# First MLP layer of a fused attention and MLP kernel: blocks of 512 tokens against whole batches

## The chip, the cores and the metric

One core of one Trainium2 chip. The metric is device time of one execution in microseconds; three runs of the kernel before took 1290.98, 1290.95 and 1288.83 us (median 1290.95).

## The reference, cut to what matters

Eight batches of 576 tokens, 512 channels, all float32. Three stages follow each other.

```
a   = softmax(phi, axis=seq)                       # 32 memories a head, 8 heads
k_m, v_m = a^T k, a^T v                            # per head 32 x 64
x   = softmax(q k_m^T / 8) v_m                     # attention output, 576 x 512 a batch
y   = x + relu(LN(x) @ w_ch1) @ w_ch2              # 512 -> 2048 -> 512: the MLP of this change
h   = gelu(y @ w_in); u, v = halves of h           # the second MLP ("phase two")
out = y + (u * (w_sg @ LN(v) + b_sg)) @ w_out
```

The weights w_ch1 and w_ch2 come as float64 and are converted on the chip.

## The kernel before, in words

Float32 products are made of three fp32r matmuls (high by high, high by low, low by high), so each operand exists as a pair of tiles, h and l. Because x is attention weights times v_m, the first layer is not computed from x: `make_vw` multiplies v_m of a batch with the centred, scaled w_ch1 (tiles VW, per batch b and block fb of 512 hidden units), and layer one multiplies VW with the attention weights aT directly. So layer one's stationary operand depends on the batch. The division by the standard deviation of x comes at the end, as a factor of the row.

**Tokens and tiles.** Two batches (a pair) make nine tiles of 128 tokens: four of the even batch, one that joins the last 64 tokens of both, four of the odd batch (`tile_rows`, L125). `phase1` runs the 36 tiles in nine blocks of four, 512 tokens. A block's aT has two tiles of 512 columns.

**Steps.** A block has 16 steps, one for each chunk c of 128 hidden units. In a step `m1` (L549) does layer one for 512 tokens into one PSUM bank ph (two such banks, L137), in pieces where the batch changes within the block (`pieces`, L537): every piece has six matmuls. Relu goes to ScalarE (hh, L563), its low part to VectorE (hl, L564). Two steps later `m2` (L567) does layer two: four tiles of 128 tokens, each three matmuls of 512 columns into a PSUM bank y0 to y3 that collects over the 16 steps (L574 to L576). After the last step VectorE scales a bank, adds x (L579) and the tile goes to y_d in DRAM.

**What sets the order.** All other work of phase one is a list of calls with due times in steps (`at_time`, L587); `run_until` issues what is due between m1 and m2 of a step. `tile_base` (L591) gives the times of the attention units: a unit (batch b, 128 tokens i, the last one 64) lays q out in DRAM (`lay_q`), loads it, transposes it on VectorE (`t_q`, L328), makes scores on TensorE (`t_scores`, L337), softmax (`t_norm`) and aT (`t_attn`). `t_x` (L442) multiplies aT with v_m for the residual x, `t_ln` takes its statistics. Batch 0's first four units run ahead of step 0 in a form of their own (`t_q0`, `t_scores0`, `t_attn0`, two units at a time). A planner under the kernel orders the instructions of each engine by its own estimate of times; all DMAs are issued on SP's queue, in order.

**Weights and room.** Raw W1 and W2 chunks and the converted W2 (16 tiles) share `wpool`, 22 tiles of 4 KB a partition; VW and the centred W1 share `wpool2`, 13 tiles, with part of VW in wpool for odd batches.

**The end of phase one.** From the last block on, `begin_phase2(n)` (L823) prepares phase two, n steps into that block: w_sg is transposed from n = 0, w_in is loaded from n = 3, w_out from n = 11, y of pair 0 comes back from DRAM from n = 9 (`y_in`), and `s2` (L786), the first product of phase two, runs for its first five tiles from n = 12. In the last block the chunks are taken in the order 12 to 15, 0 to 11, so that wpool2 comes free early. `s2` and the w_sg transposes take turns in two PSUM banks (tag v).

Of the kernel before, what the change touches and what calls it, by code (L numbers as in the profile page):

```python
# [28 lines left out]
def fused_kernel(ctx: ExitStack, tc: tile.TileContext, q, k, v, phi, g1, w1, w2, w_in, g2, w_sg, b_sg, w_out, out):  # L29
# [7 lines left out]
    P = 128  # L37
# [30 lines left out]
    es_mlp, es_w2, es_attn, es_right, es_left = ExitStack(), ExitStack(), ExitStack(), ExitStack(), ExitStack()  # L68
# [66 lines left out]
    def phase1():  # L135
# [6 lines left out]
        wpool2 = pool(es_w2, "wpool2", 13)  # L142
# [55 lines left out]
        def lay_q(u, b, i):  # L198
# [4 lines left out]
            for a in range(4):  # L203
                src = q[b].rearrange("(c o) s (e f) -> o e s c f", o=2, e=2)
                with behind_w2(TB <= u["T"]["t"] < 2 * TB, 6 + u["T"]["t"] - TB):
                    load(t[a, 0:u["n"]], src[a // 2, a % 2, i * P:min((i + 1) * P, S)])

        def load_q(u, b, i):
            n = u["n"]
            if u["T"]["t"] < TB:  # L210
# [3 lines left out]
                load(t, q[b, :, i * P:(i + 1) * P, :].rearrange("h p d -> p h d"))  # L214
# [146 lines left out]
        def t_q0(us):  # L361
            qTs = two(wpool, F32, "qT0")
            for u, qT in zip(us, qTs):
                t = u.pop("q")
                u["qT"] = qT = qT.rearrange("p (c n) -> p c n", c=4)
                pt = ps_0([P, 4, P], "ptq")
                for pr in range(4):
                    PE.transpose(pt[:, pr, :], t[:, 2 * pr:2 * pr + 2, :].rearrange("p h d -> p (h d)"), ident)
                A.copy(qT, pt)

        def t_scores0(us):
            kT = st["kT"]
            sc = ps_0([P, 2, 2, P], "sc")
# [11 lines left out]
            z, a = two(wpool, F32, "z0")  # L385
            V.transpose(out=z, in_=sc.rearrange("p t g n -> p (t g n)"))
            z3 = z.rearrange("p (b m) -> p b m", m=NM)
            m = at.tile([P, 16], F32, tag="m0", name="m0")
            V.tensor_reduce(out=m, in_=z3, axis=AX.X, op=ALU.max)
            V.tensor_tensor(out=z3, in0=z3, in1=m.unsqueeze(2).to_broadcast([P, 16, NM]), op=ALU.subtract)  # L390
            A.activation(z, z, AF.Exp, scale=SCALE)
            us[0]["z"] = (z, z3, a)

        def t_attn0(us):
            z, z3, a = us[0]["z"]
            r = at.tile([P, 16], F32, tag="r0", name="r0")
# [3 lines left out]
            V.tensor_tensor(out=z3, in0=z3, in1=r.unsqueeze(2).to_broadcast([P, 16, NM]), op=ALU.mult)  # L400
            tr = V.transpose(out=a, in_=z)
            if 0 not in aT:
                aT[0] = (
                    mo.tile([P, HK, BLK], F32R, tag="aTh", name="aTh"),
                    mo.tile([P, HK, BLK], F32R, tag="aTl", name="aTl"),
                )
            a3 = a.rearrange("p (t g n) -> p g t n", t=2, g=2)
            t0 = us[0]["T"]["t"]
            ah, al = (x[:, :, t0 * P:(t0 + 2) * P].rearrange("p g (t n) -> p g t n", t=2) for x in aT[0])
            A.copy(ah, a3)  # L410
            lo = (G if t0 == 0 else V).tensor_tensor(out=al, in0=a3, in1=ah.bitcast(F32), op=ALU.subtract)
            for u in us:
                u["T"]["tr"] = tr if t0 == 0 else lo
# [11 lines left out]
        def t_attn(u):  # L425
# [5 lines left out]
            j, tt = divmod(u["T"]["t"], TB)  # L431
            if j not in aT:
                aT[j] = (
                    mo.tile([P, HK, BLK], F32R, tag="aTh", name="aTh"),
                    mo.tile([P, HK, BLK], F32R, tag="aTl", name="aTl"),
                )
            ah, al = aT[j]
            cs = slice(tt * P + u["o"], tt * P + u["o"] + n)
# [3 lines left out]
        def t_x(T):  # L442
            j, tt = divmod(T["t"], TB)
            ah, al = aT[j]
            ts_ = slice(tt * P, (tt + 1) * P)
            T["x"] = mo.tile([P, DM], F32, tag="x", name="x", bufs=8)
            for o, m, b, _ in tile_rows(*divmod(T["t"], TPP)):
                VBh, VBl = VBs[b % 2]
                px = ps_a.tile([P, DM], F32, tag="a", name="px")
                for g in range(HK):  # L450
                    cs = slice(g * 4 * D, (g + 1) * 4 * D)
# [530 lines left out]
```

## Time and profile before

| | |
|---|---|
| three runs | 1288.83, 1290.95, 1290.98 us; median 1290.95 |
| profiled execution | span 1287.4 us from its first to its last instruction |
| TensorE busy | 1230.4 us, 96% of the span |
| VectorE, ScalarE, GpSimd busy | 679.6, 440.6, 408.6 us |
| mean granted clock of TensorE | 0.981 |
| layer one (L559) | 1536 matmuls |
| layer two (L574 to L576) | 1728 matmuls |

The profile is of one execution, taken by the hardware. Busy time is the union of an engine's instructions; matmuls overlap, so the time one of them costs is the distance from its start to the next start. The granted clock is a share of full speed: TensorE runs at 2.4 GHz (1.00) or 1.2 GHz. The time of the profiled execution itself is its span; the runs' times include what lies around the span.

### The profile page before, as it was taken

The numbers are of one execution on the slowest core, as the hardware profiler recorded it, in microseconds if no ns is written. First come the engines' busy times: TensorE is split into PE (matmuls) and PEld (weight loads), VectorE is DVE, ScalarE is ACT, GpSimd is POOL, SyncE is SP. The second block draws the span as 40 slices with busy tenths as digits, with TensorE's granted clock in tenths as the row PEclk, the third lists the DMA queues.
The fourth block names the chain that finished last, engine by engine and source line by source line (L and its number), as shares of the span: only waits on it lengthen the run. The fifth ranks groups of instructions, "written<-read, shape, count | busy, mean of one in ns | idle before, by whom it ended". The sixth has DMA issues, their size and how long they took to land.

```text
span 1287.4 us, 20559 instructions
## 1 busy us (share of the span) xinstructions
PE 1230.4 (96%) x7723; PEld 1024.8 (80%) x7723; DVE 679.6 (53%) x1472; ACT 440.6 (34%) x870; POOL 408.6 (32%) x659
## 2 busy tenths in 40 slices
PE   4589989999999999999999999999999999999998
PEld 2367667888878888788787888778998998998997
DVE  3677564445355355345354434765567547547632
ACT  2653332222223232132132123543353444434430
POOL 1144222111102111111021112514575666647641
PEclk8689989999999999999999999999999999999999
DMA  9996673164353453532431104322033024013301
GB/s 213 305 259 162 188 189 91 52 182 123 100 146 99 117 142 89 146 106 79 136 83 58 51 25 136 123 84 75 25 91 106 1 80 134 9 34 115 91 9 66
DMA packets 205076, 138.96 MB, mean 108 GB/s; under 512 B 95536, under 2 KB 176688, under 8 KB 204976
## 3 DMA queue, kind: packets, MB, share of 16 engines
q1 hardware_dynamic: 204976, 137.64, 38.4%
q8 instruction: 61, 1.00, 0.3%
q14 instruction: 39, 0.32, 0.1%
HBM read 114.53 MB, written 31.46 MB: 113 GB/s over the span
## 4 chain that ended last, share of the span: by engine, by line
PE 84%; DMA 7%; DVE 4%; SPq 2%; issue 1%; ACT 1%; POOL 1%; POOLq 0%; DVEq 0%; ACTq 0%
PE ph L559 17%; PE py L574 9%; PE py L576 9%; PE pvs L891 9%; PE py L575 9%; PE po L914 8%; PE pu L866 7%; PE pv L794 6%; DMA raw<-in_moe_w_ch_dram 4%; PE pvw L515 2%; PE sc L342 2%; SPq L80 2%; PE kvp L276 1%; DMA kv<-in_v_dram 1%; PE px L452 1%
## 5 line engine op out<-in xcount | busy, mean ns | idle before, releaser
L559 PE MATMUL ph<-aTh,vw 128*128 128x64 f32 (+7 forms) x1024 | 254.1, 318 | 10.2 <-ACT aTh L410 4.6
L574 PE MATMUL py<-whl,hh 128*128 128x512 f32 x576 | 230.3, 403 | 0.0
L575 PE MATMUL py<-whl,hh 128*128 128x512 f32 x576 | 227.5, 395 | 0.0
L576 PE MATMUL py<-whl,hl 128*128 128x512 f32 x576 | 225.6, 395 | 0.0
L559 PEld LDWEIGHTS ph<-aTh,vw 128*128 128x128 f32 x1024 | 178.2, 191 | 33.3 <-issue 7.5
L564 DVE SCALAR_TENSOR_TENSOR hl<-ph,hh 128x512 fp32r<-128x512 f32 x144 | 99.0, 687 | 169.8 <-ACT hh L563 169.5
L563 ACT ACTIVATE hh<-ph 128x512 fp32r<-128x512 f32 x144 | 86.0, 599 | 266.2 <-PE ph L559 264.9
L559 PE MATMUL ph<-aTl,vw 128*128 128x448 f32 (+7 forms) x512 | 163.7, 320 | 0.0
L574 PEld LDWEIGHTS py<-whl,hh 128*128 128x128 f32 x576 | 108.6, 188 | 30.0 <-issue 6.3
L576 PEld LDWEIGHTS py<-whl,hl 128*128 128x128 f32 x576 | 108.3, 188 | 27.9 <-issue 5.1
L421 POOL TENSOR_TENSOR z<-z,r 128x256 f32<-128x256 f32 (+1 forms) x36 | 20.5, 570 | 342.7 <-DVE r L420 278.7
L575 PEld LDWEIGHTS py<-whl,hh 128*128 128x128 f32 x576 | 108.6, 189 | 20.9 <-issue 2.1
L891 PE MATMUL pvs<-wsh,vhl 128*128 128x288 f32 x576 | 121.2, 294 | 0.0
L559 PEld LDWEIGHTS ph<-aTl,vw 128*128 128x128 f32 x512 | 97.7, 191 | 16.0 <-issue 8.6
L866 PE MATMUL pu<-yTh,whl 128*128 128x288 f32 x512 | 110.4, 295 | 0.0
L794 PE MATMUL pv<-whl,yTh 128*128 128x512 f32 x288 | 91.9, 400 | 3.8 <-DVE vg L784 3.8
L891 PEld LDWEIGHTS pvs<-wsh,vhl 128*128 128x128 f32 x576 | 94.3, 188 | 0.6
L914 PE MATMUL po<-whl,gh 128*128 128x512 f32 x288 | 90.8, 391 | 0.0
L866 PEld LDWEIGHTS pu<-yTh,whl 128*128 128x128 f32 x512 | 85.0, 188 | 1.0
L866 PE MATMUL pu<-yTl,whl 128*128 128x288 f32 x256 | 75.4, 295 | 0.0
L891 PE MATMUL pvs<-wsl,vhl 128*128 128x288 f32 x256 | 75.4, 295 | 0.0
L894 POOL TENSOR_TENSOR gt<-gt,ug 128x288 f32<-128x288 f32 x64 | 51.6, 808 | 63.7 <-DVE gt L893 62.8
(161 smaller groups left out, 2079.0 us busy)
## 6 DMA issues: line engine op xcount, KB each, us to landing
wc<-w_d SPq DMA_DIRECT2D x56, 512.0 KB, 4.9
y_d<-x SPq DMA_DIRECT2D x36, 256.0 KB, 3.9
yr<-y_d SPq DMA_DIRECT2D x36, 256.0 KB, 3.0
kv<-in_k_dram SPq DMA_DIRECT2D x32, 256.0 KB, 4.3
kv<-in_v_dram SPq DMA_DIRECT2D x32, 256.0 KB, 4.4
raw<-in_moe_w_ch_dram SPq DMA_DIRECT2D x32, 256.0 KB, 9.6
raw<-in_moe_w_ch_dram SPq DMA_DIRECT2D x16, 512.0 KB, 8.2
out_dram<-yr SPq DMA_DIRECT2D x32, 256.0 KB, 2.0
```

The costliest lines, as they stand in the source:

```text
L80: return nc.sync.dma_start(out=out_ap, in_=in_ap)
L559: PE.matmul(ph[:, c0:c1], w[:, ks], x[:, g, c0:c1], start=(n == 0), stop=(n == 3 * HK - 1))
L563: A.activation(hh, ph, AF.Relu)
L564: st["hl"] = V.scalar_tensor_tensor(out=hl, in0=ph, scalar=0.0, in1=hh.bitcast(F32), op0=ALU.max, op1=ALU.subtract)
L574: PE.matmul(py, hh[:, ts_], wh, start=start, stop=False)
L575: PE.matmul(py, hh[:, ts_], wl, start=False, stop=False)
L576: PE.matmul(py, hl[:, ts_], wh, start=False, stop=stop)
L794: PE.matmul(pv, y[:, kc, cs], w, start=(n == 0), stop=(n == 3 * KC - 1))
L866: PE.matmul(pu, w[:, ds_], y[:, kc, cs], start=(n == 0), stop=(n == 3 * KC - 1))
L891: PE.matmul(pvs, v_, w_, start=(n == 0), stop=(n == len(ops) - 1))
L894: G.tensor_tensor(out=gt, in0=gt, in1=ug, op=ALU.mult)
L914: PE.matmul(po, gg[:, dc, cs], w, start=(n == 0), stop=(n == 3 * KC - 1))
```

## The change

Layer one and two go by batches: eight blocks of 576 tokens instead of nine of 512. A step's layer one has two pieces, of 256 and 320 tokens, each in a PSUM bank of its own (the same two banks). The first 512 tokens of a batch go on to layer two as before, as four tiles. The outputs of the last 64 tokens are kept (`rems`, four tiles of wpool a pair, for 16 chunks), the even batch's in columns 0 to 63, the odd batch's in 64 to 127; when the odd batch is done, `m2_rem` does layer two for the joined tile, 48 matmuls into one bank. In the last pair these matmuls are spread over the last block's steps, in a bank of tag v.

With it: batch 0's last 64 tokens are attended ahead of step 0, as a third group; t_x stands within the batch's own block (x has seven buffers, was eight); the due times of units, W1 and W2 change; VW lies in `wearly` (6 tiles) and `wlate` (2), the centred W1 in `wcen` (5); the last block takes its chunks in plain order, and phase two's preparation begins at n = 3 instead of 0, y_in at 12 instead of 9, s2 at 13 instead of 12.

```diff
-        wpool2 = pool(es_w2, "wpool2", 13)
+        wlate = pool(es_w2, "wlate", 2)
+        wearly = pool(es_wc, "wearly", 6)
+        wcen = pool(es_wc, "wcen", 5)
...
-                h, l = two(wpool if b % 2 and fb < NFB - 1 else wpool2, F32R, "vw")
+                h, l = two(wearly if fb < NFB - 1 else wlate, F32R, "vw")
...
-        def t_x(T):
...
-            T["x"] = mo.tile([P, DM], F32, tag="x", name="x", bufs=8)
-            for o, m, b, _ in tile_rows(*divmod(T["t"], TPP)):
...
+        def t_x(T, b, i):
+            ah, al = aT[b]
+            VBh, VBl = VBs[b % 2]
+            o, n = (0, P) if i < 4 else (REM * (b % 2), REM)
+            ts_ = slice(i * P - o, i * P + n)
+            if "x" not in T:
+                T["x"] = mo.tile([P, DM], F32, tag="x", name="x", bufs=7)
...
+        hid, ybank, rems = {}, {}, {}
+        PIECES = ((0, 2 * P), (2 * P, S))
+
+        def m1(b, c):
+            ah, al = aT[b]
             fb, n = divmod(c, DM // P)
             ks = slice(n * P, (n + 1) * P)
-            ph = ps_h.tile([P, BLK], F32, tag="h", name="ph")
-            for c0, c1, b in pieces(j):
+            pair, odd = divmod(b, 2)
+            if not odd and c % 4 == 0 and (pair, c // 4) not in rems:
+                rems[pair, c // 4] = wpool.tile([P, 4, 2, P], F32R, tag="w", name="rem")
+            rem = rems[pair, c // 4][:, c % 4, :, REM * odd:REM * odd + REM]
+            hh = mo.tile([P, BLK], F32R, tag="hh", name="hh", bufs=3)
+            hl = mo.tile([P, BLK], F32R, tag="hl", name="hl", bufs=3)
+            for c0, c1 in PIECES:
+                ph = ps_h.tile([P, S - 2 * P], F32, tag="h", name="ph")[:, 0:c1 - c0]
                 n = 0
                 for g in range(HK):
                     wh, wl = VW[b, fb][g]
                     for w, x in ((wh, ah), (wh, al), (wl, ah)):
-                        PE.matmul(ph[:, c0:c1], w[:, ks], x[:, g, c0:c1], start=(n == 0), stop=(n == 3 * HK - 1))
+                        PE.matmul(ph, w[:, ks], x[:, g, c0:c1], start=(n == 0), stop=(n == 3 * HK - 1))
                         n += 1
-            A.activation(hh, ph, AF.Relu)
-            st["hl"] = V.scalar_tensor_tensor(out=hl, in0=ph, scalar=0.0, in1=hh.bitcast(F32), op0=ALU.max, op1=ALU.subtract)
-            hid[j, c] = (hh, hl)
+                outs = [(ph[:, 0:2 * P], hh[:, c0:c0 + 2 * P], hl[:, c0:c0 + 2 * P])]
+                if c1 == S:
+                    outs.append((ph[:, 2 * P:], rem[:, 0, :], rem[:, 1, :]))
+                for src, h, l in outs:
+                    A.activation(h, src, AF.Relu)
+                    st["hl"] = V.scalar_tensor_tensor(out=l, in0=src, scalar=0.0, in1=h.bitcast(F32), op0=ALU.max, op1=ALU.subtract)
+            hid[b, c] = (hh, hl)
...
+        def m2_rem(pair, c, bank):
+            if c == 0:
+                ybank["rem", pair] = bank()
+            py = ybank["rem", pair]
+            rem = rems[pair, c // 4]
+            wh, wl = W2[c]
+            PE.matmul(py, rem[:, c % 4, 0, :], wh, start=(c == 0), stop=False)
+            PE.matmul(py, rem[:, c % 4, 0, :], wl, start=False, stop=False)
+            PE.matmul(py, rem[:, c % 4, 1, :], wh, start=False, stop=(c == NF - 1))
+            if c == NF - 1:
+                t = TPP * pair + 4
+                y_of(py, tiles[t], t)
+
+        rems[0, 0] = wpool.tile([P, 4, 2, P], F32R, tag="w", name="rem")
...
+        def unit_base(b, i):
+            if b == 1:
+                return B1 + (0, 1.6, 2.6, 3.6, 4.4)[i]
+            if b == 2:
+                return 16.2 + 2.6 * i
+            return 16 * b - 18.1 + 3 * i - 0.5 * (i == 4)
...
+                x0, dx = (16 * b + 2.3, 0.25) if b == B - 1 else (16 * b + 2.4, 2)
+                at_time(x0 + dx * i, t_x, u["T"], b, i)
...
-            at_time(4 * fb - 18.5 if fb > 1 else 0.3 * fb - 26.5, load_w1, fb)
-            at_time((-16.5, -5.5, 2.6, 6.6)[fb], scale_w1, fb)
-            at_time((-16.4, -0.6, 4.0, 8.0)[fb], center_w1, fb)
-            at_time((-15, 0.8, 5.1, 9.1)[fb], make_vw, 0, fb)
+            at_time((-26.5, -26.2, -10.5, -4.5)[fb], load_w1, fb)
+            at_time((-16.5, -5.5, 1.6, 4.6)[fb], scale_w1, fb)
+            at_time((-16.4, -0.6, 2.6, 6.0)[fb], center_w1, fb)
+            at_time((-15, 0.8, 4.1, 7.6)[fb], make_vw, 0, fb)
         for c in range(NF):
-            at_time(1.1 * c - 16 if c > 2 else 0.2 * c - 26.4, load_w2, c)
+            at_time(c - 8.6 if c > 8 else 1.1 * c - 16 if c > 2 else 0.2 * c - 26.4, load_w2, c)
...
-        LAST = [*range(12, NF), *range(12)]
-        steps = [(j, c if j < NB - 1 else LAST[c]) for j in range(NB) for c in range(NF)]
+        LAST = NF * (B - 1)
+        steps = [(b, c) for b in range(B) for c in range(NF)]
+        rem_steps = list(range(NF))
...
-                m2(*steps[n - LAG], (n - LAG) % NF == 0, (n - LAG) % NF == NF - 1)
+                b, c = steps[n - LAG]
+                m2(b, c)
+                if b % 2 and b < B - 1 and c == NF - 1:
+                    for c in range(NF):
+                        m2_rem(b // 2, c, lambda: ps_y.tile([P, DM], F32, tag="y0", name="pyr"))
             run_until(n + 0.99)
-            begin_phase2(n - NF * (NB - 1))
+            begin_phase2(n - LAST)
+            for _ in range(2):
+                if n - LAST >= 4 and rem_steps and rem_steps[0] <= n - LAST - LAG:
+                    m2_rem(NPAIR - 1, rem_steps.pop(0), lambda: R["ps"].tile([P, DM], F32, tag="v", name="pyr", bufs=2))
...
-        if n == 0:
+        if n == 3:
             es_attn.close()
...
-        if n == 5:
-            es_w2.close()
+        if n == 12:
+            es_wc.close()
             R["py"] = pool(es_right, "p1y", 1, side="right")
...
-            if n == 9 + (2 * t) // 3:
+            if n == 12 + t // 2:
                 y_in(pairs[0], t)
-            if t < 5 and n == 12 + t:
+            if t < 5 and n == 13 + t:
                 s2(pairs[0], t)
```

## Rows read from the trace of the kernel before

**Rows 1.** Table of stretches: us, busy (x instructions) per engine, granted clock, DMA share, GB/s.
```profile
0.00:82.00 82.00, 44.44 (x255) 27.70 (x256) 47.95 (x87) 40.78 (x72) 13.13 (x27) 0.82 0.98 260
82.00:150.00 68.00, 67.27 (x403) 48.79 (x402) 43.66 (x87) 27.83 (x53) 27.83 (x33) 0.97 0.72 206
150.00:180.00 30.00, 22.69 (x194) 14.52 (x194) 19.36 (x53) 7.17 (x16) 9.26 (x13) 0.83 0.60 141
180.00:778.00 598.00, 596.67 (x4010) 488.79 (x4009) 274.44 (x642) 155.13 (x315) 89.32 (x187) 1.00 0.38 103
778.00:868.00 90.00, 86.58 (x382) 69.02 (x380) 59.33 (x112) 42.46 (x92) 31.57 (x37) 1.00 0.39 118
...
sum 1287.40, PE 1230.41 PEld 1024.81 DVE 679.58 ACT 440.57 POOL 408.59; mean PE 205.07 PEld 170.80 DVE 113.26 ACT 73.43 POOL 68.10
```

**Rows 2.** The chain of waits by engine, shares of the span.
```profile
PE 84%; DMA 7%; DVE 4%; SPq 2%; issue 1%; ACT 1%; POOL 1%; POOLq 0%; DVEq 0%; ACTq 0%
```

**Rows 3.** Timeline of TensorE, one step in five blocks: start us, duration us, instruction.
```profile
313.92 0.22 PE L559 MATMUL ph<-aTh,vw 128*128 128x128 f32 x1
...
315.65 0.40 PE L574 MATMUL py<-whl,hh 128*128 128x512 f32 x1
...
367.57 0.25 PE L559 MATMUL ph<-aTh,vw 128*128 128x192 f32 x1
...
369.13 0.40 PE L574 MATMUL py<-whl,hh 128*128 128x512 f32 x1
...
452.77 0.28 PE L559 MATMUL ph<-aTh,vw 128*128 128x256 f32 x1
...
454.20 0.39 PE L574 MATMUL py<-whl,hh 128*128 128x512 f32 x1
...
729.77 0.36 PE L559 MATMUL ph<-aTh,vw 128*128 128x448 f32 x1
...
731.46 0.28 PE L559 MATMUL ph<-aTh,vw 128*128 128x64 f32 x1
731.57 0.47 PE L574 MATMUL py<-whl,hh 128*128 128x512 f32 x1
...
778.44 0.39 PE L559 MATMUL ph<-aTh,vw 128*128 128x512 f32 x1
...
779.80 0.39 PE L574 MATMUL py<-whl,hh 128*128 128x512 f32 x1
```

**Rows 4.** Costliest groups, layer one's matmuls: x count, busy us, mean ns, idle before.
```profile
L559 PE MATMUL ph<-aTh,vw 128*128 128x64 f32 (+7 forms) x1024 | 254.1, 318 | 10.2 <-ACT aTh L410 4.6
...
L559 PE MATMUL ph<-aTl,vw 128*128 128x448 f32 (+7 forms) x512 | 163.7, 320 | 0.0
```

**Rows 5.** Chain of waits in phase two, one s2: start us, us, what.
```profile
1057.06 2.80 PE pv L794 x12
```

**Rows 6.** Groups by line and shape, VectorE and ScalarE passes over PSUM.
```profile
L564 DVE SCALAR_TENSOR_TENSOR hl<-ph,hh 128x512 fp32r<-128x512 f32 x144 | 99.0, 687 | 169.8 <-ACT hh L563 169.5
...
L782 DVE SCALAR_TENSOR_TENSOR z<-z,pu 128x288 f32<-128x288 f32 x64 | 28.9, 452 | 58.4 <-ACT z L781 58.0
...
L563 ACT ACTIVATE hh<-ph 128x512 fp32r<-128x512 f32 x144 | 86.0, 599 | 266.2 <-PE ph L559 264.9 <-PE py L575 0.6
```

**Rows 7.** Layer one's line: what TensorE sat idle for ahead of it (us, times).
```profile
  DVE hl L564: 6.3, 6
```

**Rows 8.** Chain of waits between the first two blocks: start us, us, what.
```profile
154.90 1.05 DVE qT L332
...
163.39 1.07 DVE qT L332
...
169.34 5.04 DMA kv<-in_v_dram
```

**Rows 9.** Waits in the last block of phase one: us in total, times, longest.
```profile
PE pv L794 <- DVE vg L784: 3.6, 2, 2.8
```

**Rows 10.** DMA issues: x count, KB each, median us from issue to landing.
```profile
raw<-in_moe_w_ch_dram SPq DMA_DIRECT2D x16, 512.0 KB, 8.2
```

More of the change, by code (lines that the diff above doesn't have):

```diff
@@ L66, in fused_kernel @@
     g2c = const.tile([P, KC], F32, name="g2c")
-    es_mlp, es_w2, es_attn, es_right, es_left = ExitStack(), ExitStack(), ExitStack(), ExitStack(), ExitStack()
+    es_mlp, es_w2, es_wc, es_attn, es_right, es_left = (ExitStack() for _ in range(6))
     def pool(es, name, bufs, **kw):
@@ L484, in scale_w1 @@
         def scale_w1(fb):
-            WC[fb] = ws = [wpool2.tile([P, 2, DM], F32, tag="w", name="wc") for _ in range(2)]
+            WC[fb] = ws = [wcen.tile([P, 2, DM], F32, tag="w", name="wc") for _ in range(2)]
             for j, raw in enumerate(raws.pop(fb)):
@@ L501, in load_wc @@
         def load_wc(fb):
-            WC[fb] = [wpool2.tile([P, 2, DM], F32, tag="w", name="wc") for _ in range(2)]
+            WC[fb] = [wcen.tile([P, 2, DM], F32, tag="w", name="wc") for _ in range(2)]
             for n in range(2):
@@ L577, in m2 @@
                 if stop:
[L578 to L580 removed]
+                    y_of(py, tiles[full(b, t)], full(b, t))
+        def m2_rem(pair, c, bank):
[11 more added lines that the diff above has]
+        rems[0, 0] = wpool.tile([P, 4, 2, P], F32R, tag="w", name="rem")
         tiles = [{"t": t} for t in range(NPAIR * TPP)]
@@ L589, in at_time, with full @@
             seq[0] += 1
-        def tile_base(t):
-            j, r = divmod(t, TB)
-            if j == 0:
-                return -17.5 + 6 * (r // 2) + 0.1 * (r % 2)
-            if j == 1:
-                return B1 + r + 0.6 * (r > 0)
-            return 16 * j - 18.1 + 3 * r
-        first_us = []
-        for b in range(B):
-            pair, odd = divmod(b, 2)
-            t0 = pair * TPP
-            items = []
-            if odd:
-                items.append((t0 + 4, 4, REM, REM))
-                items += [(t0 + 5 + i, i, 0, P) for i in range(4)]
-            else:
-                items += [(t0 + i, i, 0, P) for i in range(4)]
-                items.append((t0 + 4, 4, 0, REM))
-            first = tile_base(items[0][0])
+        def full(b, i):
+            return TPP * (b // 2) + (5 * (b % 2) + i if i < 4 else 4)
+        def unit_base(b, i):
[4 more added lines that the diff above has]
+            return 16 * b - 18.1 + 3 * i - 0.5 * (i == 4)
+        for b in range(B):
+            odd = b % 2
+            first = -17.5 if b == 0 else unit_base(b, 0)
             f = {1: F1, 2: F1}.get(b, 1.0)
@@ new lines, in phase1 @@
+            us = [
+                {"seen": set(), "E": V if i == 0 and b == 1 else G, "n": P if i < 4 else REM, "b": b, "i": i, "T": tiles[full(b, i)]}
+                for i in range(5)
+            ]
+            for i, u in enumerate(us):
+                if b == 0:
+                    at_time(-27, load_q, u, b, i)
+                    if i % 2 == 1 or i == 4:
+                        group = us[i - i % 2:i + 1]
+                        at_time(-21 + 0.1 * i, t_q0, group)
+                        at_time(-17 + 0.1 * i, t_scores0, group)
+                        at_time(-16 + 0.1 * i, t_attn0, group)
+                else:
+                    base = unit_base(b, i)
+                    at_time(base - (5.5 if i < 4 else 4), lay_q, u, b, i)
+                    at_time(base - (3.5 if i < 4 else 2), load_q, u, b, i)
+                    at_time(base, t_q, u)
+                    f = 0.7 if b == 1 else 1.0
+                    at_time(base + f, t_scores, u)
+                    at_time(base + 2 * f, t_norm, u)
+                    at_time(base + 3 * f, t_attn, u)
+                x0, dx = (16 * b + 2.3, 0.25) if b == B - 1 else (16 * b + 2.4, 2)
+                at_time(x0 + dx * i, t_x, u["T"], b, i)
+                if i in (1, 3):
+                    at_time(x0 + dx * i + 0.2, t_ln, [us[i - 1]["T"], us[i]["T"]])
+                if i == 4 and odd:
+                    at_time(x0 + dx * i + 0.2, t_ln, [u["T"]])
```

166 lines of the change are left out of this document (60 added, 106 removed).

## The prediction

> **What bounds the kernel now.** I read the table of stretches first. Between 180 and 778 us TensorE is busy 596.7 of 598 us at full granted clock, VectorE 274.4, ScalarE 155.1 and the DMA engines 0.38; from 82 to 150 us it is 67.3 of 68, in the last block of layer one (778 to 868) 86.6 of 90 [rows 1]. Only the start up to 82 us and the stretch from 150 to 180 us (22.7 of 30 us busy, clock 0.83) are bound by something else. The chain of waits says the same: 84% of the span is TensorE, 7% DMA, 4% VectorE [rows 2]. So what counts is how long TensorE needs for the instructions that change, and whether it now waits at the seams.
>
> Busy time of a matmul is no price here, since matmuls overlap: a step of 12 matmuls with 256 columns takes 1.43 us from its first start to the start of the next line, though one lasts 0.28 us. I take starts from the timeline [rows 3]. One step of layer one (six matmuls, or six and six) costs 1.36 us with 512 columns (778.44 to 779.80), 1.43 with 256+256 (452.77 to 454.20), 1.56 with 192+320 (367.57 to 369.13), 1.73 with 128+384 (313.92 to 315.65) and 1.80 with 448+64 (729.77 to 731.57). The last 64-column matmul and the next instruction are 0.11 us apart (731.46 to 731.57). 512 columns take 1.36/6 = 0.227, so 64 columns cost half of that, not an eighth: narrow pieces pay a floor.
>
> **The change part by part.** *Layer one.* Before, nine blocks of 512 tokens run 16 steps each: two blocks in one piece of 512, two each of 448+64, 384+128, 320+192, one of 256+256. That is 16 x (2 x (1.36 + 1.80 + 1.73 + 1.56) + 1.43) = 16 x 14.33 = 229.3 us, in 1024 + 512 = 1536 matmuls [rows 4]. After, 8 batches x 16 steps x 12 are again 1536 matmuls, over the same columns, but all 256 or 320 wide. Six of 256 cost half of 1.43, 0.715. Six of 320 are 1.56 less six of 192; with 192 held at the floor of 0.11 that is 0.89; by proportion between 256 and 512 columns it is 0.715 + 0.645 x 64/256 = 0.876. I take 0.89: 128 x 1.605 = 205.4 us, so **-23.9 us** (ends: -25.7 with 0.876, and -22, since one step a block is read and 0.015 us a step is 2 us in all). It lies on TensorE's dense stretches, so it is on the path; against 512 or 256+256 a step grows by 0.25 or 0.17 us, against the rest it shrinks.
>
> *Layer two.* 36 tiles x 48 matmuls of 512 columns stand before and after (8 batches x 4 tiles, and 4 joined tiles). A joined tile puts 48 into one PSUM bank in a row. Twelve into one bank take 2.80 us in phase two [rows 5], 0.233 each against 0.227: 192 x 0.006 = **+1.2 us**.
>
> *Evictions.* One pair (Relu on ScalarE, subtraction on VectorE) a step becomes three: 256, 256 and 64 columns. VectorE takes 0.687 us for 512 and 0.452 for 288 columns [rows 6], so about 0.15 + 0.00105 a column: 0.42 + 0.42 + 0.22 = 1.06 us. In all 128 x 1.06 = 135 against 99.0 us, +36 us; ScalarE (0.599 for 512) grows likewise. With VectorE 46% busy in the main stretch this is hidden, at nothing; if the cover went, 0.37 us a step would show. The new wait is on the two PSUM banks of layer one: a bank was used every second step, now every step, so a piece must be evicted within the other piece (0.9 us) and layer two (12 x 0.227 = 2.7 us), 3.6 us. The bare eviction is 0.6 + 0.7 us. TensorE waited for this subtraction 6.3 us in six places in the whole run [rows 7]. Behind a waiting matmul all of TensorE stands, layer two included. 0 to +6, I take **+1**.
>
> *Batch 0's last 64 tokens* move ahead of the first step: one q load of 128 KB (0.5 us at the 260 GB/s of the first 82 us [rows 1]), four transposes, four score matmuls, some nine small VectorE passes. The load stands on SP's queue ahead of the weight loads that bound the start. Small VectorE passes go from 0.15 us up, so nine are 1.4 to 4 us, partly beside the loads. 0 to +4, I take **+1**. W2 chunks 9 to 15 are loaded later, but keep their order among the weights: nothing, if their room is there (a rival below).
>
> *The seam before batch 1 (150 to 180 us).* There TensorE waits for attention units one after the other; their q transposes start at 154.90 and 163.39, 8.5 us apart, and a DMA for the next batch's k and v, held on SP's queue, ends the wait [rows 8]. Block 1 needed four units of batch 1 and one of batch 0, now five of batch 1, the fifth 0.8 of a step later. But its first pieces need only two of them. -5 (half of the 7.3 us of idle and more) to +8.5 (a unit), I take **+2**.
>
> *Joined tiles' bank.* The 48 matmuls take bank y0 after its last output is read, one VectorE pass of 0.7 us that was issued three tiles (2.0 us) before; the next batch's tile 0 waits for their own output, behind which a step of layer one (1.6 us) stands. Three times: 0 to +3, I take **+0.5**. The x matmuls (t_x) only move into their own batch's block: same count, 0.
>
> *The last block.* It grows on TensorE (48 matmuls of the joined tile, 11 us, and five x sets of six), while preparing phase two starts three steps later; y's first transposes at 12 instead of 9; the last s2 in the last step; and the joined tile holds one of the two banks in which s2 and the w_sg transposes alternate. Before, TensorE waited here 3.6 us for a gelu to free such a bank [rows 9]. -2 (all of it filled by the extra matmuls) to +13 (three steps of 4.3 us), I take **+3**.
>
> Phase two proper: its instructions stay, 0.
>
> Sum: -23.9 + 1.2 + 1 + 1 + 2 + 0.5 + 3 = **-15.2 us**. The profiled execution's span is 1287.4 us [rows 1]; 1272.2 after. Around it lie 3.5 us to the median of the runs shown, 1290.95; that stays. Forecast **1275.5 us**.
>
> **The rivals.** (1) *Seam*: batch 1's attention sets the time until its fifth unit: +8.5 instead of +2, and as much again if its k and v loads are late as at 169.34 [rows 8]: 1282 to 1290. For it: that stretch is a chain of single waits. Against: two units suffice to start. (2) *Evictions*: with 3.6 us instead of over a step, TensorE waits where VectorE is busiest, the weight conversions of batch 0's block (43.7 of 68 us) and the last block (59.3 of 90) [rows 1]. At 0.3 us in each of the 34 steps there and short waits elsewhere it is +10 to +14: 1285 to 1289. For it: both stretches have long VectorE passes. Against: 6.3 us in all so far.
>
> (3) *Room for W2, slower than before*: place: batch 0's block. The pool of 22 tiles (wpool) now also holds the 64-token outputs, and if a late W2 load must wait on SP's queue until the one before it is converted, seven chunks go one at a time: 8.2 us to land [rows 10] and four 512-column passes, some 2.6 us by [rows 6], 7 x 10.8 = 76 us. Seven steps there hide about 40 us (some 12 steps in 68 us). So +36: 1311. It decides from fewer than two free tiles; two at a time (38 us) are hidden. By my count of the tiles alive at step 5 (14 for W2, four of raw W1, two of outputs) two are free. Against it, narrowly.
>
> (4) *No gain*: matmul time goes by columns alone; then the sum of layer one is unchanged, as are columns and count, and only the seams count: about 0 to +8, near 1291 to 1299. Rows speak against it: 448+64 takes 0.44 us longer than 512, the same columns [rows 3]. The Trainium skill, TensorE: Matmul & The Clock Gate, section Back-to-back issue gap, gives the gap of isolated matmuls at full clock as N/2.4 + 2.5 ns, which is such a rule; by it layer one would stay as it is. The trace disagrees: 64 columns would be 29 ns, and the row has 0.11 us.
>
> **How the numbers follow.** Forecast with its own range 1263 to 1283: 0.70. Seam 0.10, evictions 0.10, W2's room 0.07, columns alone 0.03. What can be told from no change is 0.2%, 2.6 us, so faster is below 1288.4. The forecast, the seam and most of the evictions lie there: 0.87. Within: the rest of the evictions and half of (4), 0.05. Slower: (3) and half of (4), 0.08. The range 1263 to 1287 holds the forecast's cases, the seam and most evictions; its low end is the sum with -25.7, the seam at -5 and the last block at -2, short of all at once.
>
> **What would show it.** In the profile after, line by line: a step of layer one 1.60 us from first matmul to layer two, in every batch; matmuls of ph 768 of 256 and 768 of 320 columns; blocks of batches 2 to 6 without idle TensorE, each some 85 us, and 11 us more at the end of batches 1, 3 and 5. Wrong would be: idle on ph that ends with VectorE's subtraction (2); batch 1's first full step later than 190 us (1); waits on W2's loads between 100 and 150 us (3); steps of 1.8 us (4). If the last block takes over 115 us, the +3 there was too small.

## The result, and the profile after

The changed kernel took 1306.5 us (median of 4 runs, 1304.05 to 1309.65) beside 1289.89 us for the kernel before (4 runs): ratio 1.0138, interval 1.0111 to 1.0164. It is 1.4% slower, 31 us above the forecast of 1275.5 and outside its range. The profiled execution spans 1302.3 us, 14.9 more than before. First its table of stretches, cut where its own stages end (us, busy (x instructions) per engine, granted clock, DMA share, GB/s), then the chain of waits by engine.

```profile
0.00:82.00 82.00, 41.89 (x233) 26.22 (x233) 36.98 (x79) 35.10 (x67) 15.50 (x27) 0.85 1.00 244
82.00:150.00 68.00, 65.00 (x434) 48.91 (x433) 50.83 (x105) 32.82 (x72) 21.70 (x21) 1.00 0.70 209
150.00:180.00 30.00, 23.91 (x160) 17.94 (x158) 21.81 (x54) 11.42 (x30) 9.43 (x16) 0.96 0.34 87
180.00:220.00 40.00, 22.73 (x193) 14.53 (x192) 18.76 (x51) 8.61 (x24) 6.92 (x13) 0.63 0.78 198
220.00:778.00 558.00, 557.69 (x3719) 447.14 (x3718) 281.51 (x775) 169.64 (x466) 81.00 (x173) 1.00 0.37 100
778.00:882.00 104.00, 98.83 (x519) 83.34 (x519) 63.81 (x162) 49.77 (x126) 36.20 (x53) 1.00 0.36 107
882.00:1302.30 420.30, 412.48 (x2481) 375.62 (x2479) 236.46 (x497) 168.28 (x328) 237.25 (x363) 0.99 0.21 65
sum 1302.30, PE 1222.54 PEld 1013.71 DVE 710.15 ACT 475.64 POOL 408.00; mean PE 174.65 PEld 144.82 DVE 101.45 ACT 67.95 POOL 58.29
```

```profile
PE 81%; DMA 7%; DVE 3%; SPq 3%; issue 2%; ACT 2%; POOL 1%; POOLq 0%; DVEq 0%; ACTq 0%
```

TensorE is busy 7.9 us less than before (1222.5 against 1230.4) [rows 1], and its share of the chain falls from 84 to 81% [rows 2]: the work shrank and the waits grew. From 220 to 778 us TensorE stands still 0.3 of 558 us. The waits are at two places. One is the stretch from 180 to 220 us: 22.7 of 40 us busy, at a clock of 0.63. The same stretch of the kernel before:

```profile
180.00:220.00 40.00, 40.00 (x254) 33.30 (x253) 23.17 (x55) 13.92 (x30) 8.83 (x20) 1.00 0.45 115
```

Before, the hole between the first two blocks lay between 150 and 180 us [rows 1], with the second block's steps at full rate from 184; now it lies from 172 to 217, with full rate from 223. The other place is the end of phase one: from the last product of layer two to the end the run takes 420.1 us (882.2 to 1302.3), before 411.5 (875.9 to 1287.4). The last products of the two, after and before:

```profile
881.80 0.39 PE L592 MATMUL pyr<-whl,rem 128*128 128x512 f32 x1
```

```profile
875.48 0.39 PE L576 MATMUL py<-whl,hl 128*128 128x512 f32 x1
```

Four of the nine tiles of phase two's first product (s2) start before that point, from 845.6 us on; before the change it was five, from 839.3 on. One tile is 2.8 us of TensorE [rows 5], so of the 8.6 us some 2.8 are work that now stands behind the point, and the rest is waits and clock.

The predicted gain is there. A step in the timeline of TensorE after (start, duration, instruction; consecutive equal ones joined):

```profile
246.32 0.30 PE L556 MATMUL ph<-aTh,vw 128*128 128x320 f32 x1
...
247.31 0.28 PE L556 MATMUL ph<-aTl,vw 128*128 128x256 f32 x1
...
247.91 0.40 PE L578 MATMUL py<-whl,hh 128*128 128x512 f32 x1
```

That is 1.59 us (twelve matmuls, 246.32 to 247.91) where [rows 3] had 1.36 to 1.80. The groups of layer one after, from the page:

```profile
L556 PE MATMUL ph<-aTh,vw 128*128 128x256 f32 (+1 forms) x1024 | 247.5, 304 | 4.7 <-ACT vw L523 4.7
...
L563 DVE SCALAR_TENSOR_TENSOR hl<-ph,hh 128x256 fp32r<-128x256 f32 x256 | 106.8, 419 | 176.1 <-ACT hh L562 174.9
...
L556 PE MATMUL ph<-aTl,vw 128*128 128x256 f32 (+1 forms) x512 | 152.9, 299 | 0.0
```

Still 1536 matmuls, now of two shapes instead of eight [rows 4]. VectorE's pass of 256 columns takes 0.42 us [rows 6 had 0.687 for 512], 107 us in all, and 128 passes of 64 columns at 0.22 us are 28 more. The four largest of TensorE's waits between 50 and 900 us (waiter, releaser: us, times, longest):

```profile
PE py L578 <- ACT hh L562: 9.1, 8, 2.6
PE px L453 <- DVE vw L524: 7.9, 1, 7.9
PE pvw L517 <- DVE wc L500: 6.7, 1, 6.7
PE kvp L278 <- DMA kv<-in_v_dram: 6.2, 3, 3.6
```

The first line is new: layer two waits for a Relu of layer one, 4.9 us of it before 150 us and 4.2 behind 778. Before, it was layer one that waited, 2.5 us, for VectorE's subtraction to free its bank; that wait is gone. The longest of the new waits ends at 75.6 us, where the Relu stands in ScalarE's queue behind a weight conversion that waited for its load:

```profile
74.62 0.65 ACT L103 ACTIVATE raw<-raw 128x512 f32<-128x512 f32 x1 [1.50 <-DMA raw<-in_moe_w_ch_dram]
75.18 0.37 ACT L562 ACTIVATE hh<-ph 128x256 fp32r<-128x256 f32 x1
```

The wait of pvw for wc lies at 51 us, ahead of layer one's first matmul. The px line and 5.9 us of the kvp line are the hole; the chain of waits through it, start and us:

```profile
172.51 3.57 issue
...
190.99 2.86 DMA kv<-in_v_dram
193.89 1.71 PE kvp L278 x24
...
196.28 2.08 PE pvw L517 x16
...
199.71 0.72 PE sc L344 x8
...
205.18 0.32 DVE at L436
...
207.17 4.86 DMA q<-q_d
212.10 1.08 DVE qT L334
...
215.05 0.40 ACT aTh L440
215.45 0.49 ACT vw L523
```

The 0.72 us of sc at 199.71 hold the score products of batch 1's fifth unit, 64 tokens. In TensorE's queue they stand behind kvp, which are batch 2's products of k and v, and those wait until 193.9 for batch 2's loads; then they wait for a bank that a pvw of batch 1 holds. The fifth unit's attention weights are cast (written as aTh, which makes the unit ready) at 205.5, and only then can batch 1's first step finish its second piece. Then px, batch 1's residual product, waits 7.9 us for a bank that holds batch 2's pvw; the cast that frees it (vw, 215.45) stands in ScalarE's queue behind the attention weights of batch 2's first unit (215.05). Those were held up on VectorE, which stood 6.6 us for the q of batch 2's second unit (it landed at 212.0) with the first unit's softmax behind it in its queue.

### The profile page after: what moved, and what is told of

Its sections match the earlier page's. It is cut to its first block, busy times and chain, and to the rows that moved or that the text cites. A ratio compares the mean times of both kernels' runs of the same rounds, so it can differ in the third digit from the quotient of the medians.

```text
span 1302.3 us, 21130 instructions
## 1 busy us (share of the span) xinstructions
PE 1222.5 (94%) x7727; PEld 1013.7 (78%) x7727; DVE 710.1 (55%) x1719; ACT 475.6 (37%) x1111; POOL 408.0 (31%) x665
## 4 chain that ended last, share of the span: by engine, by line
PE 81%; DMA 7%; DVE 3%; SPq 3%; issue 2%; ACT 2%; POOL 1%; POOLq 0%; DVEq 0%; ACTq 0%
PE ph L556 14%; PE pvs L906 9%; PE py L578 8%; PE py L580 8%; PE py L579 8%; PE pu L881 8%; PE po L929 8%; PE pv L810 7%; DMA raw<-in_moe_w_ch_dram 5%; PE pvw L517 3%; SPq L80 3%; PE kvp L278 2%; PE sc L344 1%; DMA kv<-in_v_dram 1%; PE pyr L592 1%
## 5 line engine op out<-in xcount | busy, mean ns | idle before, releaser
L556 PE MATMUL ph<-aTh,vw 128*128 128x256 f32 (+1 forms) x1024 | 247.5, 304 | 4.7 <-ACT vw L523 4.7
L578 PE MATMUL py<-whl,hh 128*128 128x512 f32 x512 | 207.2, 406 | 9.2 <-ACT hh L562 9.1
L579 PE MATMUL py<-whl,hh 128*128 128x512 f32 x512 | 203.8, 398 | 0.0
L563 DVE SCALAR_TENSOR_TENSOR hl<-ph,hh 128x256 fp32r<-128x256 f32 x256 | 106.8, 419 | 176.1 <-ACT hh L562 174.9
L562 ACT ACTIVATE hh<-ph 128x256 fp32r<-128x256 f32 x256 | 97.9, 384 | 279.4 <-PE ph L556 278.2
L580 PE MATMUL py<-whl,hl 128*128 128x512 f32 x512 | 180.7, 399 | 0.6 <-DVE hl L563 0.6
L556 PE MATMUL ph<-aTl,vw 128*128 128x256 f32 (+1 forms) x512 | 152.9, 299 | 0.0
L578 PEld LDWEIGHTS py<-whl,hh 128*128 128x128 f32 x512 | 97.3, 190 | 41.8 <-ACT hh L562 14.3
L579 PEld LDWEIGHTS py<-whl,hh 128*128 128x128 f32 x512 | 97.1, 190 | 18.3 <-issue 2.6
L580 PEld LDWEIGHTS py<-whl,hl 128*128 128x128 f32 x512 | 92.4, 189 | 22.9 <-issue 8.0
```

The source lines that it names most:

```text
L556: PE.matmul(ph, w[:, ks], x[:, g, c0:c1], start=(n == 0), stop=(n == 3 * HK - 1))
L562: A.activation(h, src, AF.Relu)
L563: st["hl"] = V.scalar_tensor_tensor(out=l, in0=src, scalar=0.0, in1=h.bitcast(F32), op0=ALU.max, op1=ALU.subtract)
L578: PE.matmul(py, hh[:, ts_], wh, start=start, stop=False)
L579: PE.matmul(py, hh[:, ts_], wl, start=False, stop=False)
L580: PE.matmul(py, hl[:, ts_], wh, start=False, stop=stop)
```

## The experiments

All are edits of the changed kernel unless said, with the same computation. Ratios are to the kernel before, run beside each.

**e1, the width price.**

```diff
-        PIECES = ((0, 2 * P), (2 * P, S))
+        PIECES = ((0, 4 * P), (4 * P, S))
```

(the PSUM tiles of ph and the evictions follow the pieces)

> The changed kernel with layer one's two pieces cut at 512 instead of 256 columns: 512 + 64 tokens, the same 12 matmuls a step, two evictions a step instead of three. Theory of the prediction (a 64-column matmul costs half of a 512-column one, not an eighth): a layer-one step of 1.80 us instead of 1.60, so +0.2 us x 128 = about +25 us over the changed kernel, 1330 us. Rival (matmuls take time by their columns alone): within 3 us of the changed kernel's 1306.5.

1352.48 us, ratio 1.0485 (1.0448 to 1.0523): +46 over the changed kernel, nearly twice the expectation. Its timeline:

```profile
315.59 0.39 PE L556 MATMUL ph<-aTh,vw 128*128 128x512 f32 x1
...
317.09 0.39 PE L556 MATMUL ph<-aTh,vw 128*128 128x64 f32 x2
317.31 0.28 PE L556 MATMUL ph<-aTl,vw 128*128 128x64 f32 x1
317.43 0.28 PE L556 MATMUL ph<-aTh,vw 128*128 128x64 f32 x1
317.54 0.48 PE L581 MATMUL py<-whl,hl 128*128 128x512 f32 x1
```

The step is 1.95 us: 64-column matmuls start 0.11 us apart. 0.36 us x 128 = 46. The expectation had taken the 1.80 of the 448+64 step [rows 3], which has 64 columns fewer. So width is what pays, by 0.36 us a step, and the rival of columns alone is dead. The Trainium skill, TensorE: Matmul & The Clock Gate, section Back-to-back issue gap, gives N/2.4 + 2.5 ns for the gap of isolated matmuls at full clock, by which 29 ns is an estimate for 64 columns, and says itself that this counts too little at small N in a stream where every matmul has its weight load. The trace agrees with the second part: the row has 0.11 us, nearly four times the estimate.

**e2, batch 2's preparation and units later.**

```diff
-                return 16.2 + 2.6 * i
+                return 18.2 + 2.2 * i
```

(with the load of batch 3's phi and batch 2's prep_vb moved so that their buffers are free)

> The changed kernel with batch 2's preparation and attention units due two layer steps later, so that they no longer stand ahead of batch 1's last unit and of its residual product (px) in the queues of TensorE, ScalarE and GpSimd. Theory A (the hole of 172 to 218 us on TensorE is batch 1's last unit waiting behind batch 2): layer steps run at their full rate from about 205 us instead of 223, time 1288 to 1296. Rival B (batch 1's own chain of units sets the hole): full rate within 4 us of 223, time 1303 to 1309. Rival C (what is taken from this seam is paid at the next, before batch 2, whose units are now due later): full rate earlier, but a new hole before the third block at about 290 to 300 us, time 1303 or more.

1291.64 us, ratio 1.0015 (0.9998 to 1.0032): 15 us won. The third batch starts at 286.3 us instead of 300.7, and the end moves by 14. The fifth unit's cast comes at 192.6 instead of 205.5, the layer steps run at full rate from 203 instead of 223. Two of its stretches:

```profile
180.00:220.00 40.00, 29.11 (x234) 21.27 (x235) 16.90 (x46) 10.45 (x30) 8.19 (x14) 0.79 0.63 161
220.00:300.00 80.00, 80.00 (x573) 63.37 (x572) 44.89 (x131) 26.61 (x73) 16.63 (x35) 1.00 0.54 140
```

Theory A; no new hole before batch 2 (80.0 of 80 us), so not C. But some 11 us of hole remain between 180 and 220 us (29.1 of 40 busy).

**e3, weight loads later.**

```diff
-                    at_time(vw_at - (4 if fb == 0 else 1.5), load_wc, fb)
+                    at_time(vw_at - (0.5 if b == 1 else 4 if fb == 0 else 1.5), load_wc, fb)
```

> The changed kernel with batch 1's centred first-layer weights (wc) loaded half a step before their use instead of 1.5 to 4 steps, so that SyncE's queue does not stand for 6.4 and 12.5 us before a wc tile comes free with batch 1's q loads behind it. Theory A' (this wait delays batch 1's units): their first cast of attention weights falls from 167.5 to about 158 us, full rate of the layer steps comes 8 to 12 us earlier, time 1295 to 1299. Rival B' (TensorE reaches the preparation of batch 1 late anyway): casts within 3 us of 167.5, time 1303 to 1309.

1307.31 us, ratio 1.0144 (1.0111 to 1.0176), first cast at 168.5. What it was to take away is still there; the queue's waits from 100 to 215 us, of this kernel:

```profile
SPq L80 <- PE pvw L517: 17.1, 2, 12.6
```

In the changed kernel that line reads 17.8, 2, 12.5. So this tells nothing on the theory: the wait on SyncE's queue was not tried.

**e4, batch 0's third group earlier.**

```diff
+                        o = 0.2 if i == 4 else 0.1 * i
-                        at_time(-17 + 0.1 * i, t_scores0, group)
+                        at_time(-17 + o, t_scores0, group)
```

(t_attn0 alike)

> The changed kernel with batch 0's third attention group (its last 64 tokens) placed between the first and the second group instead of behind both. Theory: its casts come before 60 us instead of at 68.8 and 69.9, TensorE's two gaps of 3.8 and 2.6 us at 61 and 73 go, and the first step's second half starts at about 62 instead of 72. If the loss at the start is carried through to the end: time 1300 to 1302. Rival (the steps up to 100 us are paced by the weight loads, all 16 DMA engines are busy, and the hole before batch 1 takes the rest up): within 3 us of 1306.5.

1304.74 us, ratio 1.0130 (1.0084 to 1.0177). Its first 100 us, and those of the changed kernel:

```profile
0.00:100.00 100.00, 62.57 (x349) 41.95 (x350) 56.92 (x116) 46.05 (x91) 19.86 (x31) 0.82 0.96 251
```

```profile
0.00:100.00 100.00, 58.27 (x319) 37.44 (x320) 51.98 (x106) 44.93 (x86) 20.27 (x30) 0.88 0.98 245
```

The group's cast comes at 57.9 instead of 68.8, TensorE does 4.3 us more, as much as before the change (62.4), and the time doesn't follow: the loss at the start was real, and it is gone behind the hole (e5 tests it against e2).

**e5, e2 and e4 together.**

> Batch 2 two steps later (as in e2) and batch 0's third group between the other two (as in e4). In e4 the 4 to 5 us won by 100 us were gone by 180, in the hole before batch 1. If that hole was set by batch 2 standing ahead, and e2 has removed it, the start's gain now comes through: 1286 to 1288. Rival (the hole that e2 leaves, TensorE's 4.9 and 2.3 us gaps at 178 and 185, is set by batch 1's own preparation, which is paced by loads and not by the start): within 2 us of e2's 1291.6.

1292.27 us, ratio 1.0016 (1.0000 to 1.0032): the rival. What e2 leaves of the hole isn't set by the start either, though the fifth unit's cast comes at 190.2 instead of 192.6.

**e6, batch 1 earlier**, on e5.

```diff
-    B1, F1 = 9.2, 0.5
+    B1, F1 = 7.7, 0.5
```

> As e5, and batch 1's preparation and units due 1.5 layer steps earlier. In e2 batch 1's normalised k and v stand ready at 136.6 us and TensorE reaches their transposition at 147.6, its units' casts end at 166.9 to about 195. Theory (the units' due time in the queues sets what is left of the hole): casts some 7 us earlier, TensorE's idle between 170 and 210 falls from some 13 us to under 7, time 5 to 8 us under e5, 1279 to 1283. Rival (the earlier loads and conversions take the place of weight loads, DMA busy share 0.87 to 1.0 until 100 us, and delay batch 0's steps as much): within 2 us of e5, or slower.

1289.0 us, ratio 0.9994 (0.9972 to 1.0016), not told apart from e5; the first unit's cast comes at 170.3, later than e5's 162.7 and e2's 166.9. The rival.

**e7, the last joined tile behind the last step**, on e2: the 48 products use the bank y0, as for the other pairs, and the two chunks a step in the phase-two bank go.

```diff
-                if b % 2 and b < B - 1 and c == NF - 1:
+                if b % 2 and c == NF - 1:
...
-            for _ in range(2):
-                if n - LAST >= 4 and rem_steps and rem_steps[0] <= n - LAST - LAG:
...
```

> As e2, but the last pair's joined tile is computed behind the last step, in the bank of the first tile, as for the other pairs, instead of two chunks a step in one of the two banks that phase two's first product needs. Theory (the entry into phase two is late because that product has one bank left): the starts of its tiles before the end of layer two go from 4 to 5 or 6, time 3 to 6 us under e2. Rival (y_in's chain, from the loads of y through the DVE transpose, ScalarE's and GpSimd's casts, paces those tiles, and the 48 matmuls that come behind leave TensorE nothing to cover the last eviction): no change or up to 5 us slower.

1312.23 us, ratio 1.0169 (1.0139 to 1.0199), 20 us slower than e2, worse than its rival had it. Two of phase two's first product's nine tiles start before layer two ends (861 us), four in e2, and from 830 to 930 us TensorE waits 6.9 us on that product's own evictions, some 6 on later steps of phase two and 4.3 on the conversion of w_in. This fits the joined tile being useful cover where the change puts it, but that is argued, since the edit reorders the rest as well. Why the second tile starts 28 us behind the first is not settled; it did not wait for y, all nine tiles of which are converted by 840.3.

**e8, y_in earlier**, on e2.

```diff
-        wlate = pool(es_w2, "wlate", 2)
-        wearly = pool(es_wc, "wearly", 6)
+        wlate = pool(es_w2, "wlate", 4)
+        wearly = pool(es_wc, "wearly", 4)
...
-        if n == 12:
+        if n == 8:
...
-            if n == 12 + t // 2:
+            if n == 8 + t:
-            if t < 5 and n == 13 + t:
+            if t < 5 and n == 10 + t:
```

(make_vw takes wearly for its first two chunks)

> As e2, but the pool of the first layer's first two chunks is closed at step 8 of the last block instead of the pool of three at step 12, so that y_in of phase two starts four steps earlier and its first five tiles three steps earlier. Theory (the entry is paced by y_in's chain): five or more of the first product's tiles start before the last step's end, from the end of layer two to the end of the run falls from 420.6 us to about 412, time 1281 to 1285. Rival (the bank held by the joined tile paces them, or the loads of y collide with those of phase two's weights): within 2 us of e2.

1281.8 us, ratio 0.9940 (0.9917 to 0.9962): 10 us won. Six tiles of phase two's first product start before the end of layer two (four in e2), and from there to the end it takes 408.3 us (872.2 to 1280.5). The last product of layer two in e8, and then two stretches of TensorE around the end, first of the changed kernel and then of e8:

```profile
871.81 0.39 PE L592 MATMUL pyr<-whl,rem 128*128 128x512 f32 x1
```

```profile
840.00:880.00 40.00, 35.94 (x176) 29.36 (x175) 25.05 (x50) 20.14 (x39) 19.24 (x21) 1.00 0.23 70
880.00:920.00 40.00, 36.05 (x205) 32.00 (x204) 25.49 (x56) 14.90 (x33) 16.53 (x32) 0.91 0.28 84
```

```profile
840.00:880.00 40.00, 38.97 (x204) 32.99 (x203) 23.39 (x58) 16.70 (x41) 14.48 (x29) 1.00 0.31 90
880.00:920.00 40.00, 39.67 (x260) 36.91 (x260) 27.28 (x62) 18.23 (x43) 20.52 (x34) 1.00 0.19 58
```

The chain of waits through the entry in the changed kernel, from one y tile to the next in the same buffer:

```profile
851.46 1.57 POOL yTl L793
853.06 1.12 DVE sl L788
854.20 1.15 ACT yTh L792
...
855.42 1.58 POOL yTl L793
```

On two staging buffers two tiles take 4 us; begun at step 12 of 16, the nine are converted from 843.5 to 860.9 us (before the change from 793 to 822). The first tile of the product starts at 845.6, half a us behind the first y tile. The next ones start at 857.1, 869.3 and 878.9, long after theirs, so y_in sets the first start and not the spacing. e8 also moves the product's own due times by three steps; which of the two pays is not told apart.

**e9 to e12, what is left of the hole.** e9 joins e4, e2 and e8. e10 has on it `at_time(12.7 if (b, fb) == (1, 2) else vw_at, make_vw, b, fb)`; e11 `bufs=2` for q and `bufs=6` for x; e12 both.

> The three edits of e4, e2 and e8 together: batch 0's third group between the other two, batch 2 two steps later, y_in four steps earlier. The start's gain did not come through in e5, so the time is e8's within 2 us, 1280 to 1284; if the gains add to the start's 5 us after all, 1276 to 1279.

1280.92 us, ratio 0.9933 (0.9909 to 0.9957): e8's time.

> As e9, and batch 1's third chunk of first-layer weights (make_vw) due one step earlier, ahead of the transposition of its last two units' q. Theory (TensorE's gap of 5.2 us at 175 in e5 is that chunk's two banks waiting for VectorE's short write into them, which stands in VectorE's queue behind a transposition that waits for a q load): the gap at 175 goes, time 2 to 5 us under e9. Rival (the products behind it wait for batch 1's units all the same): gap of the same length before the next ph or sc instead, within 1.5 us of e9.

1278.67 us, ratio 0.9921 (0.9895 to 0.9948), not told apart from e9. e9's gap of 5.3 us at 177 goes, and one of 5.5 us opens at 183 ahead of ptsum, batch 2's: the rival.

> As e9, with two buffers for the q tile of a unit instead of one (paid with one x tile less), so that a unit's q load no longer waits for the transposition of the unit before. Theory (what is left of the hole before batch 1 is the chain q load 3 to 5 us, transposition, next q load, five times): the casts of batch 1's five units end at 185 or earlier instead of about 194, the hole shrinks by 5 to 10 us, time 1273 to 1278. Rival (the units wait for VectorE's and TensorE's queues, not for their loads): within 2 us of e9. Below e9 the other way: one x tile less makes px wait at a batch's start, some us slower.

1283.03 us, ratio 0.9948 (0.9928 to 0.9968): the rival.

> e10 and e11 together on e9. If the two waits are links of one chain, the gain is that of the better one; if they are two, it is their sum, 1270 to 1275. Rival: within 2 us of e9.

1282.82 us, ratio 0.9945 (0.9928 to 0.9962). The fifth unit's cast stays at 194 (191.8 in e9). Neither wait held the units, nor did both together.

**e13, all of batch 2's preparation behind batch 1's first step**, on e10.

```diff
-                return 16.2 + 2.6 * i
+                return 22.0 + 1.55 * i
...
-            f = {1: F1, 2: F1}.get(b, 1.0)
+            f = {1: F1, 2: F1, 3: 0.65}.get(b, 1.0)
```

(batch 3's phi load 1.5 ahead of its preparation, prep_vb of batch 2 at +0.3)

> As e10, with all of batch 2's preparation (softmax of phi, k and v products) and its units due behind batch 1's first layer step, about four steps later than in the changed kernel, and the preparation of batch 3 moved behind it. Theory A to its end (what is left of the hole at 172 to 205 us, TensorE's gaps ahead of pt, mb, ptsum and kvp of batch 2 at half the clock, is batch 2's preparation ahead of batch 1's first ph): these gaps go, the layer steps run at full rate from about 195, time 1268 to 1274. Rival B (batch 1's own five units end no earlier than now, so the gaps stand before ph instead): full rate within 4 us of 205, time 1276 to 1282. Rival C (batch 2 is late at its own start, at about 285 us, and what is won is paid there): a new gap of 5 us or more between 270 and 300, time 1278 or more.

1276.95 us, ratio 0.9897 (0.9857 to 0.9937). The profile decides more than the time, whose interval overlaps e10's:

```profile
175.93 0.70 PE L344 MATMUL sc<-qT,kT 128*64 128x64 f32 x8 [2.56 <-DVE qT L334]
186.13 0.85 PE L556 MATMUL ph<-aTh,vw 128*128 128x320 f32 x2 [9.51 <-ACT aTh L440]
...
189.18 0.49 PE L578 MATMUL py<-whl,hh 128*128 128x512 f32 x1
```

Batch 2 no longer stands ahead, the fifth unit's cast comes at 185.8 instead of 191.8 to 193.7 in e9 to e12, and full rate at 189. Now batch 1's own last unit ends the hole (9.5 us ahead of ph). So full rate is theory A's, the time and the gap ahead of ph are rival B's. A part of rival C came true: 1.6 us of TensorE lost from 220 to 300 us. The profiled execution is the fastest of the four (1269.9, up to 1279.6) and began layer one 4 to 7 us earlier than its siblings (51.4 us against 55.2 to 58.2 in e9 to e12), where the edit has no due time. Counted from its own first matmul of layer one, the fifth unit's cast comes 134 us later (137 in e10) and full rate 138 (147 in e10).

**e14, y_in earlier alone**, without e2.

> The changed kernel with y_in four steps earlier alone (the edit of e8 without that of e2). If the miss is the sum of the seam and of the entry into phase two, which lie 600 us apart, the edits add: e8 was 10 us under e2, so this is 10 us under the changed kernel, 1295 to 1298, and its time from the end of layer two to the end of the run is 408 to 409 us. Rival (the late entry follows from the late batches ahead of it): 1303 or more.

1293.48 us, ratio 1.0038 (1.0021 to 1.0055): 13 us under the changed kernel, somewhat more than expected, and 408.3 us behind layer two. So the gain at the end doesn't hang on the late batches: 15 us (e2) and 13 (e14) alone, 25 together (e8).

## Why the prediction was wrong, point by point

*Layer one, -23.9: right.* Steps of 1.59 to 1.60 us, 128 of them, against 229.3 us: -24.5 to -25.8, near the end that I had by proportion (0.876). e1 confirms the price of width by itself. The gain is there on the chip; it was paid back at the two ends of phase one, most of it ahead of 220 us: until then TensorE is busy 153.5 us, before the change 174.4 (sums of the stretches shown).

*Layer two, +1.2, and joined tiles' bank, +0.5: nothing.* A joined tile's matmuls start 0.227 us apart (498.42 to 499.10 us for three), as the others do, and from 220 to 778 us TensorE stands still 0.3 us in all.

*The seam, "-5 ... to +8.5 (a unit), I take +2": the step that failed.* I priced the fifth unit alone, by the spacing of units before. Rival (1) had the right place and the wrong size. What I left out is who else stands in the queues there: batch 2's preparation was due at steps 10.7 to 15.7, and batch 1's fifth unit's attention at 15.7, so on queues that run in order the unit waited for the next batch's loads, and px for the next batch's banks (the chain above: kvp until 193.9, sc of the fifth unit at 199.7, px 7.9 us). The diff had both due times. That "two units suffice to start" was true and useless: the first piece started at 180 and the second waited until 206. My own test (first full step later than 190 us) came out at 223. e2 took 15 us back by one edit of due times; in e13, with all of batch 2 behind, full rate comes at 189, some 34 us sooner than in the changed kernel, 7 of them from an earlier start of layer one, and 5 behind the kernel before.

*Batch 0's last 64 tokens, +1: mis-sized, without effect.* They cost 4 us of TensorE's work by 100 us (58.3 against 62.4), 3 more than I took. e4 gives them back and e5, against e2, shows nothing of it in the time.

*Evictions, +1 (0 to +6): at the edge, by another way.* VectorE's 135 us came out as worked out. The wait grew by some 7 us (9.1 against 2.5), none of it between 220 and 778 us. It lies in the two stretches that rival (2) named, at half its price, but it is not its wait: layer one no longer waits for VectorE to free a bank. Layer two waits for Relus that stand in ScalarE's queue, before 150 us mostly behind a weight conversion that waits for its load (75.6, 98.4 and 108.4 us: 4.4 of the 4.9), behind 778 behind gelus and conversions of phase two. I had also misread the 6.3 us in six places [rows 7]: they count matmuls and weight loads apart, of matmuls alone it was 2.5 us in three.

*Last block, +3 (-2 to +13): a little small, for another reason.* From the start of the last block to the end of the run TensorE stands still 10.1 us before the change (778.4 to 1287.4) and 13.0 after (774.1 to 1302.3), and the granted clock falls to 0.91 from 882 to 920 us. I had put it on the bank that the joined tile holds; e7 gives that bank back and loses 20 us. e8 and e14 win 10 to 13 us by an earlier y_in and earlier due times of the product behind it. That is more than the change had cost there: in e8 TensorE stands still 5.9 us over the same stretch (761.9 to 1280.5). Whether the kernel before would gain by the same edit was not tried, so these 10 to 13 us are not the size of the miss.

*W2's room (3) and columns alone (4)*: none of TensorE's waits after is on W2's loads directly, and by way of ScalarE's conversions (above) weight loads cost some 4 us, not 36; that 1306.5 lies near (3)'s 1311 is chance. e1 rules out (4).

*The sum*: 1272.2 + 3.5 is 1275.7, not 1275.5, and of the 3.5 us only 1.8 lie around a span (1304.05 against 1302.3 in the profiled execution); the rest was the spread of the runs. Neither matters beside 31 us.

With both ends edited (e9: 1280.9, e13: 1277.0) the kernel comes within 1.5 to 5.4 us of the forecast of 1275.5. That doesn't make the forecast right, and the nearness is in part luck, since the edit at the end gives back more than the change had cost. e13 is 1.0% faster than before and, by the two ratios, 2.4% faster than the changed kernel.

What stays open: what spaces batch 1's five units 6 to 8 us apart in e13 (not the q buffer, e11, nor the place of the pvw in the queues, e10); the waits on SyncE's queue for a free weight tile were not tried; and at the end, y_in's due time and that of the first product behind it were only moved together.

## What to carry to other kernels

The saving on the dense stretch of the bound engine arrived in every step, but not in the time, because the work that must be ready at the ends of that stretch was not ready. For each block, list what the first step needs last, and everything with a due time ahead of it on each queue that runs in order, the next block's preparation above all. A due time that was harmless while a block needed four units of its batch cost 15 us here when it needed five. Where the profile has a stretch bound by single waits, one more such wait (my +8.5, at the top of a range) was not the most that it could cost.

## What the runs showed of the hardware

The hole cost twice here, by TensorE's waits and by its clock. In the changed kernel the granted clock is 0.63 on the mean of 180 to 220 us: in this run of waits, of 1 to 8 us each, much of the work runs at the lower of the two levels (1.2 GHz), and matmuls of 256 columns that take 1.43 us for twelve at the upper one [rows 3], 0.12 each, start 0.22 apart (207.47 and 207.69):

```profile
207.47 0.41 PE L556 MATMUL ph<-aTl,vw 128*128 128x256 f32 x1
207.69 0.41 PE L556 MATMUL ph<-aTh,vw 128*128 128x256 f32 x1
...
216.72 0.58 PE L453 MATMUL px<-VBh,aTh 128*128 128x256 f32 x1 [7.86 <-DVE vw L524]
```

And the load-bound start differs between executions: with the same due times up to there, layer one began at 57.7 to 60.4 us in six profiled executions (the changed kernel, e2, e3, e7, e8 and e14).
